# Layer 2's first down projection in seven products for four pairs of tiles, and seven tests moved

## The chip, the cores and the metric

One Trainium2 chip, of which the kernel uses one core. The metric is the device time of one execution, in microseconds (us). The engines are named as the profile names them: PE is the matrix engine (TensorE), DVE the vector engine, ACT the scalar engine, POOL the engine called GpSimd, SP the engine that issues most of the transfers. Each works through its own queue in the order in which the program was written; semaphores make one wait for another.

## The reference

Two layers, each a Fourier mixing step and a gated block, both added to x (2048 tokens of 640 features; the gated block has 1728 hidden features):

```python
x = x + _A_ref(_layernorm(x), dft_seq_re, dft_seq_im, dft_hid_re, dft_hid_im)
x = x + _B_ref(_layernorm(x), w_gate, w_up, w_down)
...
def _B_ref(x, w_gate, w_up, w_down):
    g = jnp.einsum("bsd,df->bsf", x, w_gate)
    u = jnp.einsum("bsd,df->bsf", x, w_up)
    h = _sigmoid(g) * u
    return jnp.einsum("bsf,fd->bsd", h, w_down)
```

`_A_ref` is Re(DFT_seq(DFT_hidden(x))) with the DFT matrices given as inputs. The change touches the last product of `_B_ref`, called "down" here, and the place of some work on the inputs.

## The kernel before, in words

**Precision.** Each operand is kept as two 16-bit parts, high and low, and each product is made of three matmuls (high by high, high by low, low by high). To make the parts of a value, ACT writes the high one and DVE the low one as the difference.

**Blocks, tiles and steps.** The tokens are worked on in four blocks of 512 (b = 0 to 3), each of four row groups of 128. The hidden features make 13 tiles of 128 (j = 0 to 12) and a short one (j = 13, "the tail", 64 wide). For each block there is a stretch of gate and up products, one unit of steps for each tile (units 0 to 13 of the block), and then the down product in eight steps (units 14 to 21). The number of a job in the code, `block[0] + 13.6` for example, is a place in this count: it says between which matmuls the job is written, and so where it stands in the queue of its engine. It is no time.

**Gate and up.** `seven(b, j)` makes gate and up of two tiles with seven products for eight (a scheme of Strassen's kind: some operands are sums, and products serve several results). It interleaves four places for jobs (`some(0)` to `some(3)`) with its parts: `part_one` to `part_seven` are PE's, `gate` is ACT's sigmoid, `up` (L1600, L1602) DVE's two multiplications, `part_seven` and `part_three` end with DVE's L1572 and L1580, and `up_parts` splits the finished tile. The results of two tiles are finished only in the next step. The last call has tile 12 alone, works off what is left, and does the tail (`gate_tail`, L1726 to L1730).

**Down, plain.** `down` takes the row groups one after another: 14 tiles, three matmuls a tile (two for the tail), two column halves of 320: 328 matmuls for a block (L1743). Each half ends in an add to x on DVE (L1758).

**Down, in seven products.** Where `(layer, b)` is in `MADE`, tiles 2m and 2m+1 form a pair m (0 to 5), whose hidden features are a 2 by 2 matrix of halves of 256 tokens. `mated_down` multiplies it by the pair's weights with seven products, called A11, A12, A22 and S1 to S4. For that, `mates_sums` makes four sums of a pair (L1629 to L1632, DVE) and `mates_parts` splits them: hA for the products A11 and A12, hS for S1 and S2, hR for S3 and S4, hB for A22 (L1640 on ACT, L1641 on DVE; hB is 256 wide, the others 512). hA comes with the pair's second tile, the rest in `mates_rest` one step later; the last pair's rest is written behind the 38th entry of down. The products are chained in PSUM banks: A11 in bank "a" is added to x by DVE (L1808), then S2 goes on in the same bank, is added, then S3, then A22; S1 and S4 share bank "d" in the same way. A product that goes on in a bank must wait for the add before it. The tiles without a partner (12 and 13 before) go in as plain matmuls (L1799). In layer 2, blocks 1, 2 and 3 are done so: 252 + 40 = 292 matmuls a block. The pair's summed weights ("T", 640 KB a pair) are loaded by `load_t` on SP.

**Work that rides along.** In layer 2's block 0 the Fourier step's results for row groups q = 1 to 3 are still being put together on DVE: `combine` (L1288), `join_hidden` (L1302 or L1304, with L1214 and L1215) and `add_hidden` (L1323), six jobs for each q. During a block's down the next block's operands are prepared, for two pairs of row groups: `pair_apply` (L655), `pair_combine` (L662 to L665), `pair_parts` (L673 on ACT, L674 on DVE) and `pair_transpose` (SP, L680). The kernel relies on symmetries of the DFT matrices, and 84 **tests** check these on the inputs all through the program: POOL loads rows of `in_ct` (L1916: four transfers for a test), DVE folds them (L1922, L1923, L1925), ACT sums the squares (L1888). A tuple of `TESTS` is (layer, block, place of the load, of the folding, of the sum). Similar tests look at `in_wh`. Ten tests stood in the down of layer 1's last block, ten in layer 2's block 0.

**From layer to layer.** Layer 2 begins with the Fourier step. Its first products need the last rows of layer 1, by way of DVE's add (L1758), statistics, POOL, ACT and DVE again: L939 (ACT) and L949 (DVE) write what PE's L1088 reads.

Of the kernel before, what the change touches and what calls it, by code (L numbers as in the profile page):

```python
# [18 lines left out]
D = 640  # L19
# [61 lines left out]
NP = 6  # L81
MADE = {(1, 1), (1, 2), (1, 3)}
TESTS = [(0, 1, 3.5, 4.9, 5.7), (0, 1, 4.5, 5.9, 6.7), (0, 1, 5.5, 7.1, 7.9), (0, 1, 7.38, 8.97, 9.78), (0, 1, 9.25, 10.85, 11.65), (0, 1, 11.12, 12.72, 13.53),
# [195 lines left out]
def folded(ctx, tc, pool, dram, big, acc, flag, homes, x, ct, wh, wg, wu, wc, wd, out):  # L279
# [66 lines left out]
    def at(u, f, *a):  # L346
        jobs[max(0, int(u // 1))].append((u, f, a))
# [1302 lines left out]

    def seven(b, j, mated=False):

# [23 lines left out]
        def mm(some):  # L1676
            ps, k = bank() if last else (None, None)
            for i in js:
                part_one(b, i, mated and i < 2 * NP)
            for i in js:  # L1680
# [86 lines left out]

    def mated_down(b, store):

        accs = {}  # L1770
        last = b == NB - 1

        def left(m, q, hp, p):
# [8 lines left out]
        def products_of(p, n, q, w, start, stop):  # L1782
            out = [(m, hp, wp) for m in range(NP) for hp, wps in PASSES for wp in wps]

            def one(k, m, hp, wp):
                if (p, n) not in accs:
                    accs[p, n] = bank()
                nc.tensor.matmul(accs[p, n][0][:, :EH], left(m, q, hp, p), right(m, w, wp), start=start and k == 0,  # L1788
                                 stop=stop and k == len(out) - 1, skip_group_check=True)

            return [(one, k, *t) for k, t in enumerate(out)]

        def plain(p, n, g, e, start):
            out = [(j, hp, wp) for j in range(2 * NP, NF + 1) for hp, wps in (PASSES if j < NF else PASSES[:1]) for wp in wps]
# [22 lines left out]
        def done(name):  # L1817
            for m in range(NP):
                drop(name, 2 * m)
# [4 lines left out]
        for p in range(2):  # L1824
            todo += products_of(p, "c", A12, 1, True, False)
        todo += [(done, "hA")]
        for p in range(2):
            todo += products_of(p, "a", S2, 4, False, True) + [(add, p, "a", p, 1, False)]
        for p in range(2):
            todo += plain(p, "c", p, 0, False) + [(add, p, "c", p, 0, True)]  # L1830
            todo += [(put, p, slice(0, EH))] if last and p == GA else []
        for p in range(2):
            todo += products_of(p, "d", S1, 3, True, True) + [(add, p, "d", p + 2, 1, False)]
        todo += [(done, "hS")]
        for p in range(2):
            todo += products_of(p, "a", S3, 5, False, True) + [(add, p, "a", p + 2, 1, False)]
        for p in range(2):
            todo += plain(p, "e", p + 2, 1, True) + [(add, p, "e", p + 2, 1, True)]
            todo += [(put, p + 2, slice(EH, D))] if last and p + 2 == GD else []
        for p in range(2):  # L1840
            todo += products_of(p, "a", A22, 6, False, False) + plain(p, "a", p + 2, 0, False)
            todo += [(add, p, "a", p + 2, 0, True)] + ([(put, p + 2, slice(0, EH if last and p + 2 == GD else D))] if last or p else [])
            todo += [(done, "hB")] if p else []
            q = 1 - p
            todo += products_of(q, "d", S4, 2, False, False) + plain(q, "d", q, 1, False)
            todo += [(add, q, "d", q, 1, True)] + ([(put, q, slice(EH if last and q == GA else 0, D))] if last or p else [])
        marks = [n for n, t in enumerate(todo) if t[0].__name__ == "one"]
        cuts = [0] + [marks[len(marks) * k // 8] for k in range(1, 8)] + [len(todo)]

        def step(k):  # L1850
# [11 lines left out]
            def post():  # L1862
                if k < 7:
                    return
                done("hR")
                for j in range(2 * NP, NF + 1):
                    drop("ht", j)
# [238 lines left out]
    for layer in range(2):  # L2106
# [11 lines left out]
        for b in range(NB):  # L2118
            block.append(len(steps) - 3 * (b == 0))
            for j in range(3 * (b == 0), NF + 1):  # L2120
                plain = b == 0 and (first or j < 4)
                steps.append(gate_up(b, j) if plain else seven(b, j, (layer, b) in MADE) if j % 2 == 0 else None)
            if first and b == last:
# [8 lines left out]
            if (layer, b) in MADE:  # L2132
                steps += mated_down(b, not first)
        end = len(steps)
# [75 lines left out]
        for q in range(1, NB):  # L2210
            for n, (f, *a) in enumerate(((combine, 0), (combine, 1), (join_hidden, 0), (add_hidden, 0), (join_hidden, 1),
                                         (add_hidden, 1))):
                at(block[0] + 1.6 + 0.8 * n if q == 1 else block[0] + (9.6 if q == 2 else 15.6) + n, f, q, *a)
        for b in range(1, NB):
# [52 lines left out]
        for m in range(NP):  # L2267
# [7 lines left out]
            else:  # L2275
                at(block[1] + (7.6, 9.6, -3.4, -2.8, -2.2, 0.6)[m], load_t, m)
        for b in range(1, NB if first else 2):
            at(block[b] - 8.1, slots.now)
        if not first:
            at(block[1] - 8, slots.hole, XU + XTU, XTU)  # L2280
            for b in range(NB - 1):
# [205 lines left out]
```

## Time and profile before

| | |
|---|---|
| time, median of 3 runs | 1126.85 us (1126.62 to 1129.57) |
| the profiled execution | 1127.29 us, its span 1125.5 us |
| instructions in the span | 23738 |
| mean granted PE clock | 0.997 |
| HBM read, written | 180.90 MB, 29.37 MB |
| layer 2, block 0: the steps of `seven` | 657 to 713.5 us |
| layer 2, block 0: down | 713.5 to 758.1 us |
| layer 2, block 1: down | 839.1 to 878.8 us |
| layer 1, block 3: down | 553.5 to 598.1 us |

The span runs from the first to the last instruction of one profiled execution; the time of that execution is 1.8 us longer. Rows of the profile give a start, a duration, the engine, the line in the code and the operation; "out<-in" names the tiles, and nearly all of them are parts of one large buffer, "big", "acc" being a bank of PSUM. A bracket such as [0.92 <-ACT big L1616] says how long the engine stood idle before the row, and which instruction released it. In rows of a window (A:B) the columns are its length, the busy time of PE, PEld (PE's weight loads), DVE, ACT and POOL with their instructions, the granted clock of PE as a share of full speed, the share of the DMA engines' time and GB/s.

### The profile page before, as it was taken

How to read it: one execution, taken by the hardware profiler on the slowest of the kernel's cores; microseconds unless marked ns; L12 is line 12 of the kernel's file. 1: busy time of each engine (PE TensorE's matmuls, PEld its weight loads, DVE VectorE, ACT ScalarE, POOL GpSimd, SP SyncE). 2: the span in 40 equal slices, each digit the busy share in tenths (PEclk: the TensorE clock that was granted, in tenths of full speed). 3: DMA queues.
4: the chain of work that ended last, by engine and by line, in shares of the span. 5: the costliest groups of instructions: out<-in, count | busy, mean ns of one | idle time of the engine just before them, and what ended most of it. 6: DMA issues, size and time to landing. Idle time of an engine off the chain costs nothing. (4 is left out here: it accounts for less than half of the span.)

```text
span 1125.5 us, 23738 instructions
## 1 busy us (share of the span) xinstructions
PE 1104.8 (98%) x9004; PEld 881.6 (78%) x9004; DVE 827.2 (73%) x1841; ACT 532.0 (47%) x1153; POOL 345.7 (31%) x568
## 2 busy tenths in 40 slices
PE   7999999999999999999999999999999999999997
PEld 5767446788878887788877878778887888788875
DVE  7984987868877898686568877864887398827962
ACT  6975584245534654255434734422652255415530
POOL 1001654342555445243480202433530214011001
PEclk9999999999999999999999999999999999999999
DMA  7533886889598969977761674598857873398401
GB/s 237 196 103 105 303 295 208 256 260 297 204 220 245 284 208 223 266 258 240 188 200 34 183 201 160 141 254 293 258 153 157 297 244 80 99 259 232 156 7 45
DMA packets 158050, 226.54 MB, mean 201 GB/s; under 512 B 75055, under 2 KB 100161, under 8 KB 157926
## 3 DMA queue, kind: packets, MB, share of 16 engines
q1 hardware_dynamic: 139222, 176.84, 52.3%
q0 software_dynamic: 18560, 47.93, 14.8%
q8 instruction: 72, 1.18, 0.4%
q14 instruction: 52, 0.43, 0.1%
q10 hardware_dynamic: 144, 0.16, 0.0%
HBM read 180.90 MB, written 29.37 MB: 187 GB/s over the span
## 5 line engine op out<-in xcount | busy, mean ns | idle before, releaser
L1531 PE MATMUL acc<-big 128*128 128x256 f16 x4698 | 516.8, 273 | 0.8 <-DMA big<-kept_w 0.4
L1531 PEld LDWEIGHTS <-big 128*128 128x128 f16 x4698 | 459.6, 98 | 55.6 <-issue 0.8
L1916 POOL DMA_DIRECT2D big<-in_ct x256 | 174.3, 687 | 209.5 <-DVE big L1925 121.4
L1743 PE MATMUL acc<-big 128*128 128x320 f16 x1640 | 223.6, 299 | 0.0
L1535 ACT ACTIVATE big<-acc 128x256 f32<-128x256 f32 x268 | 100.7, 381 | 231.4 <-PE acc L1531 220.8
L1743 PEld LDWEIGHTS <-big 128*128 128x128 f16 x1640 | 160.5, 98 | 62.2
L1888 ACT ACTIVATE big<-big 128x768 f32<-128x768 f32 (+9 forms) x110 | 81.3, 739 | 77.6 <-DVE big L1925 61.8
L1484 PE MATMUL acc<-big 128*128 128x256 f16 (+1 forms) x705 | 114.7, 325 | 0.3 <-ACT big L730 0.3
L1788 PE MATMUL acc<-big 128*128 128x320 f16 x756 | 105.6, 299 | 0.0
L1484 PEld LDWEIGHTS <-big 128*128 128x128 f16 x705 | 68.9, 98 | 44.9 <-issue 0.6
L1788 PEld LDWEIGHTS <-big 128*128 128x128 f16 x756 | 74.0, 98 | 28.6
L323 DVE SCALAR_TENSOR_TENSOR big<-big 128x640 f16<-128x640 f32 (+8 forms) x88 | 72.1, 848 | 15.7 <-ACT big L321 10.0
L1589 ACT ACTIVATE big<-big 128x512 f32<-128x512 f32 x87 | 52.8, 628 | 63.1 <-DVE big L1580 62.8
L321 ACT ACTIVATE big<-big 128x640 f16<-128x640 f32 (+8 forms) x88 | 58.6, 698 | 24.6 <-POOL big L1390 10.9
L1600 DVE SCALAR_TENSOR_TENSOR big<-acc,big 128x256 f32<-128x256 f32 x87 | 36.3, 418 | 43.2 <-PE acc L1531 38.6
L1617 DVE TENSOR_TENSOR big<-big 128x512 f16<-128x512 f32 x51 | 35.2, 689 | 42.0 <-ACT big L1616 41.1
L1580 DVE TENSOR_TENSOR big<-big,acc 128x512 f32<-128x512 f32 x87 | 56.2, 679 | 3.2 <-PE acc L1531 2.9
L1808 DVE SCALAR_TENSOR_TENSOR big<-acc,big 128x320 f32<-128x320 f32 x48 | 23.0, 487 | 44.7 <-PE acc L1799 33.1
L494 POOL DMA_INDIRECT out<-big,rows x8 | 8.8, 1105 | 140.5 <-DMA out<-big 53.5
L1641 DVE TENSOR_TENSOR big<-big 128x512 f16<-128x512 f32 x72 | 41.2, 617 | 9.9 <-ACT big L1640 9.9
L673 ACT ACTIVATE big<-big 128x384 f16<-128x384 f32 (+2 forms) x48 | 28.6, 647 | 41.3 <-DVE big L655 29.2
L1572 DVE TENSOR_TENSOR big<-acc,big 128x256 f32<-128x256 f32 x80 | 30.4, 415 | 23.8 <-PE acc L1531 20.8
(268 smaller groups left out, 1312.4 us busy)
## 6 DMA issues: line engine op xcount, KB each, us to landing
big<-kept_s SPq DMA_DIRECT2D x84, 512.0 KB
big<-kept_w SPq DMA_DIRECT2D x115, 320.0 KB
big<-in_ct POOLq DMA_DIRECT2D x256, 128.0 KB, 5.2
big<-kept_w SPq DMA_DIRECT2D x74, 192.0 KB
kept_w<-big SPq DMA_DIRECT2D x27, 320.0 KB
big<-in_ct POOLq DMA_DIRECT2D x32, 256.0 KB, 5.7
big<-in_wd SPq DMA_DIRECT2D x25, 320.0 KB
kept_s<-big SPq DMA_DIRECT2D x13, 512.0 KB
```

Source lines behind the costliest of these rows:

```text
L321: nc.scalar.activation(dh, src, AF.Copy, scale=s)
L323: nc.vector.scalar_tensor_tensor(dl, src, s, dh, op0=OP.mult, op1=OP.subtract)
L1484: nc.tensor.matmul(ps, w[wp][:, d * P : (d + 1) * P], xt[:, xp, :], start=(d == 0 and wp == HI and xp == HI), stop=(d == ND - 1 and wp == LO))
L1531: nc.tensor.matmul(ps, wt, xt, start=start and n == 0, stop=n == len(todo) - 1, skip_group_check=not start)
L1535: nc.scalar.activation(dst, ps, AF.Copy)
L1580: nc.vector.tensor_tensor(v[1], v[1], both, op=OP.add)
L1589: nc.scalar.activation(v, v, AF.Sigmoid, scale=SG)
L1641: nc.vector.tensor_tensor(l, src, h, op=OP.subtract)
L1743: nc.tensor.matmul(held["pd", e][0][:, :EH], held["ht", j].parts[hp][:, i * P : (i + 1) * P], held["w", 2, j].parts[wp][:, e * EH : (e + 1 ...
L1788: nc.tensor.matmul(accs[p, n][0][:, :EH], left(m, q, hp, p), right(m, w, wp), start=start and k == 0, stop=stop and k == len(out) - 1, ski ...
L1888: nc.scalar.activation(v, v, AF.Square, accum_out=new_sum()[:p])
L1916: nc.gpsimd.dma_start(v[:, g], bass.AP(ct.tensor, (r * S + row) * S, [[P, NS], [d * S, 16], [1, P]]))
```

## The change

Layer 2's block 0 joins the blocks whose down is made in seven products, for the pairs 2 to 5 alone (tiles 4 to 11); tiles 0 to 3, 12 and 13 stay single. In this block the singles' products are placed between the products that go on in one bank (behind A12 and behind S1), and the last products come in another order (both S4 first, then both A22). The summed weights of pairs 2 to 5 are loaded earlier, into room that is opened for it during the block; the block's rows are stored as in the other blocks done so, two of the row groups after the end of down. The next block's operands are prepared at the places that go with this kind of down, a little later in the order. The hidden step's jobs for q = 3 in layer 2 stand two places earlier (13.6 to 18.6 for 15.6 to 20.6). Of the ten tests in layer 1's last down four go, and the six that stay stand further apart; of five in the gate and up steps of layer 2's block 0 three go; seven stand now in block 1's down.

```diff
-MADE = {(1, 1), (1, 2), (1, 3)}
+MADE = {(1, 0): range(2, NP), (1, 1): range(NP), (1, 2): range(NP), (1, 3): range(NP)}
...
-         ... (0, 3, 15.6, 16.3, 16.8), (0, 3, 16.1, 16.8, 17.3), (0, 3, 16.6, 17.3, 17.8),
-         (0, 3, 17.1, 17.8, 18.3), (0, 3, 17.6, 18.3, 18.8), (0, 3, 18.1, 18.8, 19.3), (0, 3, 18.6, 19.3, 19.8), (0, 3, 19.1, 19.8, 20.3), (0, 3, 19.6, 20.3, 20.8),
-         (0, 3, 20.1, 20.8, 21.3), (1, 0, 6.0, 8.0, 8.8), (1, 0, 7.4, 9.4, 10.2), (1, 0, 8.8, 10.8, 11.6), (1, 0, 10.2, 12.2, 13.0), (1, 0, 11.6, 13.6, 14.4),
+         ... (0, 3, 15.6, 16.6, 17.1), (0, 3, 16.4, 17.4, 17.9), (0, 3, 17.2, 18.2, 18.7),
+         (0, 3, 18.0, 19.0, 19.5), (0, 3, 18.8, 19.8, 20.3), (0, 3, 19.6, 20.6, 21.1), (1, 0, 7.0, 9.0, 9.8), (1, 0, 10.0, 12.0, 12.8), ...
+         ... (1, 1, 14.0, 15.7, 16.6), (1, 1, 15.0, 16.7, 17.6), (1, 1, 16.0, 17.7, 18.6), (1, 1, 17.0, 18.7, 19.6),
+         (1, 1, 18.0, 19.7, 20.6), (1, 1, 19.0, 20.7, 21.6), (1, 1, 20.0, 21.7, 22.6), ...
...
-                part_one(b, i, mated and i < 2 * NP)
+                part_one(b, i, i // 2 in pairs)
...
-    def mated_down(b, store):
+    def mated_down(b, store, pairs):
...
+        single = [j for j in range(NF + 1) if j // 2 not in pairs]
...
+        singles = [], []
+        for p in range(2):
+            singles[0].extend(plain(p, "c", p, 0, False) + [(add, p, "c", p, 0, True)])
...
+        for p in range(2):
+            singles[1].extend(plain(p, "e", p + 2, 1, True) + [(add, p, "e", p + 2, 1, True)])
...
+        if b == 0:
+            todo += singles[0]
         for p in range(2):
             todo += products_of(p, "a", S2, 4, False, True) + [(add, p, "a", p, 1, False)]
+        if b:
+            todo += singles[0]
         for p in range(2):
             todo += products_of(p, "d", S1, 3, True, True) + [(add, p, "d", p + 2, 1, False)]
         todo += [(done, "hS")]
+        if b == 0:
+            todo += singles[1]
         for p in range(2):
             todo += products_of(p, "a", S3, 5, False, True) + [(add, p, "a", p + 2, 1, False)]
+        if b:
+            todo += singles[1]
+        ends = [], []
         for p in range(2):
...
+            if b:
+                todo += ends[0] + ends[1]
+                ends = [], []
+        todo += ends[1] + ends[0]
...
-                at(block[0] + 1.6 + 0.8 * n if q == 1 else block[0] + (9.6 if q == 2 else 15.6) + n, f, q, *a)
+                at(block[0] + 1.6 + 0.8 * n if q == 1 else block[0] + (9.6 if q == 2 else 15.6 if first else 13.6) + n, f, q, *a)
...
-                at(block[1] + (7.6, 9.6, -3.4, -2.8, -2.2, 0.6)[m], load_t, m)
+                at(block[1] + (7.6, 9.6, -11, -7.9, -7.6, -8.7)[m], load_t, m)
...
+            at(block[0] + 3, slots.hole, XU + XTU, FT * 2)
+            at(block[1] - 8, slots.close, XU + XTU)
```

More of the change, by code (lines that the diff above doesn't have):

```diff
@@ L1649, in mates_rest, with seven @@
             drop("hs", j)
-    def seven(b, j, mated=False):
+    def seven(b, j, pairs=()):
         js = [j, j + 1] if j + 1 < NF else [j]
@@ L1782, in products_of @@
         def products_of(p, n, q, w, start, stop):
-            out = [(m, hp, wp) for m in range(NP) for hp, wps in PASSES for wp in wps]
+            out = [(m, hp, wp) for m in pairs for hp, wps in PASSES for wp in wps]
             def one(k, m, hp, wp):
@@ L1793, in plain @@
         def plain(p, n, g, e, start):
-            out = [(j, hp, wp) for j in range(2 * NP, NF + 1) for hp, wps in (PASSES if j < NF else PASSES[:1]) for wp in wps]
+            out = [(j, hp, wp) for j in single for hp, wps in (PASSES if j < NF else PASSES[:1]) for wp in wps]
             def one(k, j, hp, wp):
@@ L1817, in done @@
         def done(name):
-            for m in range(NP):
+            for m in pairs:
                 drop(name, 2 * m)
@@ L1826, in mated_down @@
         todo += [(done, "hA")]
+        singles = [], []
+        for p in range(2):
+            singles[0].extend(plain(p, "c", p, 0, False) + [(add, p, "c", p, 0, True)])
+            singles[0].extend([(put, p, slice(0, EH))] if last and p == GA else [])
+        for p in range(2):
+            singles[1].extend(plain(p, "e", p + 2, 1, True) + [(add, p, "e", p + 2, 1, True)])
+            singles[1].extend([(put, p + 2, slice(EH, D))] if last and p + 2 == GD else [])
+        if b == 0:
+            todo += singles[0]
         for p in range(2):
             todo += products_of(p, "a", S2, 4, False, True) + [(add, p, "a", p, 1, False)]
-        for p in range(2):
-            todo += plain(p, "c", p, 0, False) + [(add, p, "c", p, 0, True)]
-            todo += [(put, p, slice(0, EH))] if last and p == GA else []
+        if b:
+            todo += singles[0]
         for p in range(2):
@@ L1834, in mated_down @@
         todo += [(done, "hS")]
+        if b == 0:
+            todo += singles[1]
         for p in range(2):
             todo += products_of(p, "a", S3, 5, False, True) + [(add, p, "a", p + 2, 1, False)]
+        if b:
+            todo += singles[1]
+        ends = [], []
         for p in range(2):
[L1838 to L1843, printed above, removed]
-            q = 1 - p
-            todo += products_of(q, "d", S4, 2, False, False) + plain(q, "d", q, 1, False)
-            todo += [(add, q, "d", q, 1, True)] + ([(put, q, slice(EH if last and q == GA else 0, D))] if last or p else [])
+            ends[0].extend(products_of(p, "a", A22, 6, False, False) + plain(p, "a", p + 2, 0, False))
+            ends[0].extend([(add, p, "a", p + 2, 0, True)])
+            ends[0].extend([(put, p + 2, slice(0, EH if last and p + 2 == GD else D))] if last or p else [])
+            ends[0].extend([(done, "hB")] if p else [])
+            q = 1 - p
+            ends[1].extend(products_of(q, "d", S4, 2, False, False) + plain(q, "d", q, 1, False))
+            ends[1].extend([(add, q, "d", q, 1, True)])
+            ends[1].extend([(put, q, slice(EH if last and q == GA else 0, D))] if last or p else [])
+            if b:
+                todo += ends[0] + ends[1]
+                ends = [], []
+        todo += ends[1] + ends[0]
         marks = [n for n, t in enumerate(todo) if t[0].__name__ == "one"]
@@ L1865, in post @@
                 done("hR")
-                for j in range(2 * NP, NF + 1):
+                for j in single:
                     drop("ht", j)
@@ L2121, in folded @@
                 plain = b == 0 and (first or j < 4)
-                steps.append(gate_up(b, j) if plain else seven(b, j, (layer, b) in MADE) if j % 2 == 0 else None)
+                steps.append(gate_up(b, j) if plain else seven(b, j, MADE.get((layer, b), ())) if j % 2 == 0 else None)
             if first and b == last:
@@ L2132, in folded @@
             if (layer, b) in MADE:
-                steps += mated_down(b, not first)
+                steps += mated_down(b, not first, MADE[layer, b])
         end = len(steps)
```

10 rows, old and new, of the table TESTS are left out of this document.

## The prediction

> **What bounds the kernel now.** I read the first part of the profile's page, then the chain that ended last, then TensorE's waits after the opening, then VectorE in order of time.
>
> ```profile
> PE 1104.8 (98%) x9004; PEld 881.6 (78%) x9004; DVE 827.2 (73%) x1841; ACT 532.0 (47%) x1153; POOL 345.7 (31%) x568
> 713.71 44.55 PE acc L1743 x328
> PE acc L1088 <- ACT big L939: 1.4, 1, 1.4
> PE acc L1531 <- DMA big<-kept_w: 0.4, 1, 0.4
> ```
>
> TensorE is busy 98% of the span, and after the opening hardly anything makes it wait. So a matmul less is worth its slot, as long as nothing new makes TensorE wait. The second row is the stage that changes: layer 2's first down, 328 matmuls in 44.55 us, 0.1358 us each. But a 98% engine hides how close the next one is. VectorE (DVE) has 73% over the span, and around this down it has no rest:
>
> ```profile
> 687.92 0.69 DVE L1617 TENSOR_TENSOR big<-big 128x512 f16<-128x512 f32 x1 [3.77 <-ACT big L1616]
> ...
> 701.59 0.75 DVE L1572 TENSOR_TENSOR big<-acc,big 128x256 f32<-128x256 f32 x2
> ...
> 712.72 0.69 DVE L1617 TENSOR_TENSOR big<-big 128x512 f16<-128x512 f32 x1 [0.92 <-ACT big L1616]
> 713.44 0.69 DVE L1727 SCALAR_TENSOR_TENSOR big<-acc,big 64x512 f32<-64x512 f32 x1
> ...
> 715.53 0.83 DVE L1304 SCALAR_TENSOR_TENSOR big<-big 128x644 f32<-128x644 f32 x1
> ...
> 717.33 0.42 DVE L1922 TENSOR_TENSOR big<-big 128x256 f32<-128x256 f32 x1
> ...
> 718.53 0.42 DVE L1578 TENSOR_TENSOR big<-big 128x256 f32<-128x256 f32 x1
> ...
> 721.93 0.69 DVE L1617 TENSOR_TENSOR big<-big 128x512 f16<-128x512 f32 x1 [0.74 <-ACT big L1616]
> ```
>
> From 687.92 to 712.72 nothing but the queue itself sets when an instruction starts (the one other wait there is 0.19). The last row makes the low half of tile 12, ready at 722.6. Down starts at 713.55 and reads it at its 73rd matmul, at 723.3: 0.7 us to spare, 8 us after down began. VectorE is already that far behind TensorE.
>
> **The change part by part.** *Matmuls.* Four pairs by seven products: 7 x 2 halves x 4 pairs x 3 passes = 168. Singles: five full tiles x 3 + 2 = 17, on 4 row groups x 2 column halves = 136. Together 304, 24 fewer: **-3.26 us**. The mixed kind of down issues at the same slot in block 1 (108 matmuls in 14.67 us by the chain), so this term is sure; the counts follow from the loops, and that the change leaves them as they were is no case to weigh.
>
> *VectorE's queue in layer 2, block 0.* Prices, from block 1, which does all this today:
>
> ```profile
> 843.68 0.42 DVE L1629 TENSOR_TENSOR big<-big 128x256 f32<-128x256 f32 x1
> ...
> 845.14 0.41 DVE L1600 SCALAR_TENSOR_TENSOR big<-acc,big 128x256 f32<-128x256 f32 x1
> ...
> 847.24 0.88 DVE L1808 SCALAR_TENSOR_TENSOR big<-acc,big 128x320 f32<-128x320 f32 x2
> 848.04 1.62 DVE L1641 TENSOR_TENSOR big<-big 128x512 f16<-128x512 f32 x3
> 849.58 1.13 DVE L655 TENSOR_SCALAR big<-big,small 128x640 f32<-128x640 f32 x2
> ...
> 852.35 1.75 DVE L674 TENSOR_TENSOR big<-big 128x384 f16<-128x384 f32 x3
> ```
>
> From start to start: a pair's four sums 1.46, its three late parts (hS, hR, hB) 1.54, an add 0.40, apply and combine of a row pair of the next block 2.77, its first three parts 1.67. From the first fence: a test 1.20, a join 1.80, the tail 2.09 with its wait; a combine is two additions of 128x322, 0.8. Of the 1.54, a 512 part is 0.60 and the 256 part 0.34; hA and the part of a tile that isn't paired are 512 parts too, an up is two halves of 0.33.
>
> Now the queue, in the order of the code. In the step of tiles 8 and 9, three parts (1.54) stand at 687.9 for a part and an up (1.28): 0.26 late. In the step of tiles 10 and 11, sums and parts come (3.00), a test and a half-tile part go (1.80): 1.5 late, so the L1572 of 701.59 ends tile 10 at 703.4. TensorE needs that at 704.1: still no wait. In tile 12's step another 1.46 of sums comes, tile 10's half-tile part goes (0.8 with its wait): tile 11's up, which ended at 711.8 (712.72 less the wait of 0.92), ends at 713.8. Three parts (1.54) and hA (0.60) follow: the pair 10/11's hA is ready at 715.9. The first product reads its low half at its 12th matmul, at 715.0: **0.9**.
>
> Then tail 2.09, join 1.80, the combine moved up to 13.6 (0.8, for a test of 1.20 that goes), 1.05 for L1578 and L1580, sums 1.46, up 0.67, a wait on ACT of 0.71: tile 12's high half at 724.3, its low half at 725.0. The singles, now in front of S2, read it at matmuls 61 and 63: 722.6. **2.1** (1.7 and 0.4).
>
> From 725.0 these stand ahead of the add that ends S2: two adds 0.8, late parts 1.54, combine 0.8, L1323 pair 1.54, apply and combine 2.77, test 1.20, join 1.80, parts 1.67, test 1.20, fourth part 0.87, two adds 0.8; with the add itself 15.4: 740.4. TensorE reaches S3, which goes on in the same bank, 102 matmuls after 725.0, at 738.9: **1.5**; the second half finds another L1323 pair ahead of its add: **0.3**. S4 waits likewise for S1's second add, behind apply and combine (2.77) and an add: 745.8 against 743.9: **1.9**. After that it is even. In all **+6.7**, so this stage ends 3.5 later, not 3.3 earlier. Bounds: 0, if the queue is reached earlier by as much as it is lengthened; 10, if waits on reused room, which no row shows, come on top. I take the walk, since by the same walk the rows of before come out within half a microsecond.
>
> *ACT and the transfers.* ACT has one 512 and one 256 activation more per pair and is idle half of this stage: nothing. Four loads of the paired weights (640 KB each, on SP) go from 750 and 765 to before and about the start of down:
>
> ```profile
> 710.00:720.00 10.00, 10.00 (x79) 7.56 (x78) 7.69 (x16) 4.21 (x9) 5.42 (x12) 1.00 0.30 99
> ```
>
> They come into a stretch at DMA share 0.30 and are first read at about 728, so they cost nothing; without cover one costs the 3 us that 640 KB take at 200 GB/s. They leave the stretch after 750, at whose end TensorE waits 0.4 for weights (first fence): **-0.4** (0 to -0.4). Stores of the block's rows come later, behind all this.
>
> *Seven tests out of layer 1's end and this block, into block 1's down.* Two places. First, the end of layer 1, where four of ten tests go:
>
> ```profile
> 574.87 16.16 POOL L1916 DMA_DIRECT2D big<-in_ct  x24
> 601.11 0.47 DVE L1758 SCALAR_TENSOR_TENSOR big<-acc,big 128x320 f32<-128x320 f32 x1
> 599.65 6.07 PE L1088 MATMUL acc<-big 128*128 128x256 f16 x54
> 607.13 0.39 PE L1088 MATMUL acc<-big 128*128 128x256 f16 x2 [1.42 <-ACT big L939]
> 608.02 3.05 PE L1088 MATMUL acc<-big 128*128 128x256 f16 x16 [0.50 <-DVE big L949]
> 605.00:610.00 5.00, 2.97 (x21) 1.79 (x19) 4.14 (x10) 3.25 (x8) 0.00 (x0) 0.92 0.01 3
> 610.00:615.00 5.00, 5.00 (x41) 3.95 (x39) 3.84 (x8) 4.09 (x10) 0.00 (x0) 0.74 0.00 0
> ```
>
> The last add (601.11) runs 2.8 us after its product (598.1 plus 0.2), because VectorE's queue is full of tests whose data POOL issues at 2.7 us a test until 591. Everything up to L939 and L949 hangs on that add. Four tests fewer are 4.8 of VectorE and 10.8 of POOL: the add comes on time, both waits end 2.8 earlier, before TensorE gets there at 605.7. That gives back 2.1 (605.7 to 608.0, less two matmuls). The granted clock then fell (0.92 and 0.74 in these slices, 5 x 0.08 + 5 x 0.26 = 1.7 us lost), because of this hole; that goes too. 3.8, of which I take **-3.5**, since a small wait may show up behind (bounds 0, if the queue stays late, and -4.1).
>
> A rule speaks on the clock. The Trainium skill (TensorE: Matmul & The Clock Gate, Part 1) has the clock drop after a whole idle window of about 3.4 us. By it a hole of 2.1 us would cost only itself, here and in the down, and the sum would lose 1.7 of that gain. The trace differs: the hole above held two matmuls and the clock still fell.
>
> Second, block 1's down:
>
> ```profile
> 861.18 1.29 DVE L674 TENSOR_TENSOR big<-big 128x384 f16<-128x384 f32 x2 [1.97 <-DMA big<-big]
> 864.52 1.07 DVE L1808 SCALAR_TENSOR_TENSOR big<-acc,big 128x320 f32<-128x320 f32 x2
> 866.26 2.61 PE L1788 MATMUL acc<-big 128*128 128x320 f16 x18
> ```
>
> Three tests (3.6) come ahead of S3's add at 864.52, with an idle 1.97 to take them up: 1.6 late or more, against 1.3 to spare before the matmul of 866.26. **+0.8** (0 to 2.3, the latter if the idle moves along).
>
> **Sum:** -3.26 + 6.7 - 0.4 - 3.5 + 0.8 = +0.3. The profiled execution took 1127.29 (span 1125.5 and 1.8 around it), so 1127.6; the median shown is 0.44 lower than that execution: **1127.1**.
>
> **Rivals.** (1) *VectorE keeps up*: the down's holes don't come, the rest does: -3.26 - 0.4 - 3.5, 1119.7. For it: the kernel's holds elsewhere cost nothing at 0.7 spare; in block 1 hA comes 1.4 after the start of down and still in time. Against: there fewer additions stand in tile 12's step, and six pairs give hA 15 matmuls, four only 9. Half of the holes gives 1123.0. (2) *Slower: tests' data late.* VectorE waits for the data of the last tests of this down, with the adds of S3 now queued behind:
>
> ```profile
> 742.24 0.42 DVE L1923 TENSOR_TENSOR big<-big 128x256 f32<-128x256 f32 x1 [2.38 <-DMA big<-in_ct]
> 748.46 0.43 DVE L1923 TENSOR_TENSOR big<-big 128x256 f32<-128x256 f32 x1 [1.56 <-DMA big<-in_ct]
> ```
>
> Before, only adds with a whole product's time to spare stood behind such waits. If both recur ahead of S3's adds, which are just in time, that is 4 more: 1131.1. It decides where data land after VectorE gets to them, about 746 and 752. Against: VectorE gets there later than before. (3) *The clock halves in the down*, after the 2.1 or the 1.9: 1.7 each; the first is taken up by the waits behind it, the second not: 1128.8, and 1130.5 if another follows.
>
> **How the numbers follow.** Forecast 0.40; rival 1 0.28; rival 2 0.20; rival 3 0.12, a third of it beyond 0.3%. About 0.3% (3.4 us) is what a measurement here tells from no change: faster means below 1123.5, slower above 1130.2. So faster 0.28, same 0.48, slower 0.24. The forecast's own range is 1124 to 1130; with most of rivals 1 and 2, and with the layer's end giving nothing back (1130.6), the range is 1120 to 1133.
>
> **What would show it.** Right: 304 matmuls in layer 2's first down, four holes there, before the third pair's end of A11, in the first singles, at S3 and at S4, put down to L1641, L1616/L1617 and L1808; no wait on L939 and no half clock near 605 to 613; VectorE busy without rest from 689 to 746. Wrong: a down of 41.3 us with no hole, or the hole at 607 still there.

## The result, and the profile after

The changed kernel takes **1152.53 us** (median of 4 runs, 1148.93 to 1155.01), the kernel before 1126.73 in the same series (4 runs): ratio **1.0228, 95% interval 1.0212 to 1.0244**, slower, and far above the upper end of the forecast range (1133). The profiled execution took 1150.57 us, its span 1148.7, that is 23.2 us more than the 1125.5 of before. TensorE's waits in that span, longest sum first (engine, tile, line, what it waited for: us in total, times, longest):

```profile
PE acc L1531 <- ACT big L1535: 7.9, 3, 6.6
PE acc L1789 <- DVE big L1809: 6.8, 2, 4.8
...
PE acc L1531 <- DMA big<-big: 4.4, 1, 4.4
PE acc L1800 <- ACT big L1616: 1.9, 1, 1.9
```

(In the changed kernel the product of a pair is L1789, a single's L1800, the add to x L1809, tile parts L1616, L1617 as before.) Before, TensorE's longest wait after the opening was 1.4 us. To see where the waits lie, I cut both spans at the first product of each stage of layer 2; lengths in us:

| stage | before | after | difference |
|---|---|---|---|
| Fourier step, from L1088 on | 57.60 | 53.49 | -4.1 |
| block 0, down | 44.55 | 48.73 | +4.2 |
| block 1, steps | 81.00 | 88.85 | +7.9 |
| block 1, down | 39.66 | 47.55 | +7.9 |
| block 2, steps | 79.91 | 86.28 | +6.4 |
| block 3, steps | 80.14 | 81.19 | +1.1 |

The other stages differ by 0.3 or less. The stage that was rewritten lost 4.2; **22.1 us were lost in three stages whose own matmuls the change leaves alone**. Three places follow, each shown by TensorE and by what released it.

**Block 0's down.** TensorE in order of time (start, us, engine, line, operation, tiles, count, idle before and who ended it), then slices of 5 us with the columns explained under "Time and profile before":

```profile
711.47 5.20 PE L1789 MATMUL acc<-big 128*128 128x320 f16 x37 [0.43 <-DVE big L1641]
...
720.20 0.45 PE L1800 MATMUL acc<-big 128*128 128x320 f16 x2 [1.89 <-ACT big L1616]
720.92 4.56 PE L1800 MATMUL acc<-big 128*128 128x320 f16 x20 [0.28 <-DVE big L1617]
...
741.96 1.79 PE L1789 MATMUL acc<-big 128*128 128x320 f16 x12 [2.06 <-DVE big L1809]
```

```profile
605.00:610.00 5.00, 5.00 (x50) 4.23 (x48) 4.75 (x11) 3.81 (x11) 0.00 (x0) 1.00 0.01 3
...
720.00:725.00 5.00, 4.52 (x20) 2.55 (x21) 4.83 (x10) 1.49 (x4) 0.00 (x0) 0.66 0.01 3
...
740.00:745.00 5.00, 3.04 (x23) 2.20 (x23) 4.83 (x12) 2.25 (x5) 0.68 (x1) 1.00 0.99 295
```

Four holes, 4.66 us together. Behind the second and third the granted clock is 0.66 in the slice: twenty matmuls took 4.56 us for 2.72 (0.1358 each). The first slice is the end of the layer change, where before stood 0.92 and a hole: now 1.00 and none.

**Block 1's steps.** First ACT in the kernel before, then SP, POOL, ACT and TensorE of the changed kernel, picked in order of time:

```profile
768.78 0.38 ACT L1535 ACTIVATE big<-acc 128x256 f32<-128x256 f32 x1 [4.20 <-PE acc L1531]
```

```profile
759.68 1.29 SPq L499 DMA_DIRECT2D out<-big  x2
...
768.49 1.11 POOL L494 DMA_INDIRECT out<-big,rows  x1 [21.45 <-DVE big L1580]
772.26 0.98 POOL L494 DMA_INDIRECT out<-big,rows  x1 [2.66 <-issue]
...
778.64 0.66 ACT L1535 ACTIVATE big<-acc 128x256 f32<-128x256 f32 x2 [13.93 <-DMA out<-big,rows]
779.08 6.09 PE L1531 MATMUL acc<-big 128*128 128x256 f16 x39 [6.60 <-ACT big L1535]
```

Before, ACT's copy waited 4.20 us, for TensorE's product alone. Now ACT stood idle for 13.93 us until a store of block 0's rows had landed: its copy of a product goes into room that these rows had held. TensorE stood idle for 6.60 of that, because its bank came free too late (last row); the slices 770 to 780 and 780 to 790 then show a granted clock of 0.79 and 0.87.

**Block 1's down and block 2's start.** The kernel before and then the changed one: SP's transpositions of the next block's operands, VectorE and TensorE.

```profile
853.33 5.08 SPq L680 DMA_TRANSPOSE big<-big  x2
861.57 10.55 SPq L680 DMA_TRANSPOSE big<-big  x2
...
878.76 26.47 PE L1531 MATMUL acc<-big 128*128 128x256 f16 x241
```

```profile
861.11 7.08 SPq L680 DMA_TRANSPOSE big<-big  x2
871.40 17.60 SPq L680 DMA_TRANSPOSE big<-big  x2
...
873.83 1.29 DVE L674 TENSOR_TENSOR big<-big 128x384 f16<-128x384 f32 x2 [4.50 <-DMA big<-big]
...
878.91 4.96 PE L1789 MATMUL acc<-big 128*128 128x320 f16 x18 [4.79 <-DVE big L1809]
898.97 6.20 PE L1531 MATMUL acc<-big 128*128 128x256 f16 x42 [4.36 <-DMA big<-big]
```

```profile
880.00:885.00 5.00, 5.00 (x21) 2.76 (x20) 2.41 (x8) 1.88 (x4) 4.16 (x7) 0.51 1.30 153
```

The down begins at 839.10 before and 846.79 after, so the first pair of transpositions is issued at the same place (14.2 and 14.3 us into the stage). But VectorE's next L674, which overwrites what they read, is released 7.9 us after their issue before (861.18) and 12.7 after. The second pair is handed out over 17.60 us for 10.55, and its data are in place only 27.6 us after its own issue began (898.97); before it was at most 17.2 us, since block 2 started without a wait at 878.76. Each of the two holes is followed by a slow stretch, 0.51 in the slice behind the first.

### The profile page after: what moved, and what is told of

It is laid out like the page before. It is cut to its first block, busy times and chain, and to the rows that moved or that the text cites. A ratio compares the mean times of both kernels' runs of the same rounds, so it can differ in the third digit from the quotient of the medians.

```text
span 1148.7 us, 23714 instructions
## 1 busy us (share of the span) xinstructions
PE 1108.7 (97%) x8980; PEld 881.2 (77%) x8980; DVE 839.5 (73%) x1873; ACT 533.7 (46%) x1161; POOL 346.6 (30%) x568
## 5 line engine op out<-in xcount | busy, mean ns | idle before, releaser
L1531 PEld LDWEIGHTS <-big 128*128 128x128 f16 x4698 | 461.2, 98 | 69.3 <-issue 13.5
L1933 POOL DMA_DIRECT2D big<-in_ct x256 | 174.9, 689 | 208.2 <-DVE big L1942 102.2
L1535 ACT ACTIVATE big<-acc 128x256 f32<-128x256 f32 x268 | 99.6, 381 | 224.0 <-PE acc L1531 200.5
L1743 PE MATMUL acc<-big 128*128 128x320 f16 x1312 | 178.9, 299 | 0.0
L1743 PEld LDWEIGHTS <-big 128*128 128x128 f16 x1312 | 128.4, 98 | 49.8
L1789 PE MATMUL acc<-big 128*128 128x320 f16 x924 | 132.3, 302 | 7.3 <-DVE big L1809 6.8
L1789 PEld LDWEIGHTS <-big 128*128 128x128 f16 x924 | 91.1, 99 | 44.7 <-issue 7.5
L1905 ACT ACTIVATE big<-big 128x768 f32<-128x768 f32 (+9 forms) x110 | 81.5, 741 | 93.5 <-DVE big L1942 66.0
L1484 PEld LDWEIGHTS <-big 128*128 128x128 f16 x705 | 68.9, 98 | 44.9 <-issue 0.6
L1809 DVE SCALAR_TENSOR_TENSOR big<-acc,big 128x320 f32<-128x320 f32 x64 | 30.1, 486 | 40.5 <-PE acc L1800 29.0
L1580 DVE TENSOR_TENSOR big<-big,acc 128x512 f32<-128x512 f32 x87 | 56.3, 680 | 3.4 <-PE acc L1531 3.2
L1641 DVE TENSOR_TENSOR big<-big 128x512 f16<-128x512 f32 x88 | 50.4, 617 | 10.4 <-ACT big L1640 10.4
L1617 DVE TENSOR_TENSOR big<-big 128x512 f16<-128x512 f32 x43 | 29.7, 690 | 32.8 <-ACT big L1616 32.0
L1950 POOL DMA_DIRECT2D big<-in_ct x40 | 27.5, 691 | 71.2 <-ACT big L1535 44.7
```

Source lines behind the costliest of these rows:

```text
L1484: nc.tensor.matmul(ps, w[wp][:, d * P : (d + 1) * P], xt[:, xp, :], start=(d == 0 and wp == HI and xp == HI), stop=(d == ND - 1 and wp == LO))
L1531: nc.tensor.matmul(ps, wt, xt, start=start and n == 0, stop=n == len(todo) - 1, skip_group_check=not start)
L1535: nc.scalar.activation(dst, ps, AF.Copy)
L1580: nc.vector.tensor_tensor(v[1], v[1], both, op=OP.add)
L1641: nc.vector.tensor_tensor(l, src, h, op=OP.subtract)
L1743: nc.tensor.matmul(held["pd", e][0][:, :EH], held["ht", j].parts[hp][:, i * P : (i + 1) * P], held["w", 2, j].parts[wp][:, e * EH : (e + 1 ...
```

## The experiments

Twelve kernels; "A", "B" and "C" name the three places: the seven tests of block 1's down, the stores of block 0's rows, VectorE's queue in block 0's down. Stage lengths (us) from each profiled run:

| run | Fourier | b0 down | b1 steps | b1 down | b2 steps | b3 steps | median time | ratio to before (95%) |
|---|---|---|---|---|---|---|---|---|
| e1 | 53.49 | 48.54 | 87.72 | 39.67 | 79.91 | 81.89 | 1142.17 | 1.0131 (1.0115 to 1.0148) |
| e2 | 53.49 | 48.52 | 90.66 | 46.31 | 86.81 | 80.91 | 1152.85 | 1.0229 (1.0211 to 1.0246) |
| e3 | 53.50 | 44.55 | 80.12 | 46.01 | 86.62 | 79.97 | 1135.05 | 1.0065 (1.0048 to 1.0082) |
| e4 | 53.50 | 44.55 | 80.10 | 39.67 | 79.91 | 79.97 | 1125.49 | 0.9981 (0.9971 to 0.9990) |
| e5 | 53.50 | 48.53 | 86.10 | 47.31 | 85.92 | 80.64 | 1149.98 | 1.0210 (1.0193 to 1.0227) |
| e6 | 54.82 | 50.82 | 80.30 | 39.66 | 79.91 | 82.35 | 1142.30 | 1.0153 (1.0123 to 1.0183) |
| e7 | 53.49 | 46.27 | 80.09 | 39.66 | 79.91 | 80.86 | 1140.90 | 1.0130 (1.0113 to 1.0147) |
| e8 | 53.49 | 44.56 | 80.21 | 39.67 | 79.91 | 80.07 | 1123.29 | 0.9969 (0.9958 to 0.9980) |
| e9 | 53.48 | 48.91 | 80.85 | 40.00 | 92.97 | 81.09 | 1143.11 | 1.0143 (1.0125 to 1.0162) |
| e10 | 53.48 | 50.12 | 87.72 | 43.75 | 87.09 | 80.67 | 1151.40 | 1.0232 (1.0198 to 1.0265) |
| e11 | 53.48 | 50.12 | 90.48 | 39.99 | 79.91 | 82.32 | 1139.18 | 1.0103 (1.0079 to 1.0128) |
| e12 | 53.48 | 48.49 | 81.47 | 39.66 | 79.91 | 86.35 | 1136.79 | 1.0076 (1.0051 to 1.0101) |

### A: the seven tests alone, and without them (e1, e3)

e1, the changed kernel with

```diff
-(1, 1, 14.0, 15.7, 16.6), (1, 1, 15.0, 16.7, 17.6), (1, 1, 16.0, 17.7, 18.6),
+(1, 3, 10.6, 12.1, 12.8), (1, 3, 11.3, 12.8, 13.5), (1, 3, 12.0, 13.5, 14.2),
...
```

> The changed kernel with its seven tests of block 1's down moved behind block 3's step of tile 10 (seven places in block 3 of layer 2), nothing else touched. Theory A: these tests, by their transfers and by their 1.2 us each on VectorE, make the hole of 4.8 us in block 1's down, the half clock behind it and the late transposition at block 2's start; without them block 1's down goes from 47.6 back to about 39.7 us and block 2's steps from 86.3 to about 80, so -14.3: about 1138 us. Rival A': the down in seven products with its own later preparation makes them late; then the two holes stay and the time stays at 1150 or above.

1142.17 us. Block 1's down and block 2's steps are back at 39.67 and 79.91: 7.88 + 6.37 = 14.25 regained, as expected. The time fell by only 10.4, because the tests cost something at their new place: block 3's down, behind them, took 42.70 us for 39.82 (four holes of 0.21 to 0.89), and its steps 0.7 more.

e3, the kernel before with the changed kernel's list of tests:

```diff
-         (0, 3, 17.1, 17.8, 18.3), (0, 3, 17.6, 18.3, 18.8), (0, 3, 18.1, 18.8, 19.3),
...
+         (1, 1, 18.0, 19.7, 20.6), (1, 1, 19.0, 20.7, 21.6), (1, 1, 20.0, 21.7, 22.6),
```

> The kernel before with the changed kernel's list of tests and nothing else of the change (so four out of layer 1's end, three out of block 0's steps, seven into block 1's down). Theory A says that the seven cost the same 14.3 us beside the old down of block 0, and layer 1's end gives 4.3 back: about 1136.7 us. If the seven only hurt together with the new down, layer 1's end alone is seen: about 1122.4 us.

1135.05 us. With the old down of block 0 the two holes are there in full (4.63 and 3.91 us): block 1's down 6.4 longer, block 2's steps 6.7, 13.1 together; the Fourier step gives 4.1 and block 1's steps 0.9. So the seven tests need nothing else of the change to do their harm.

### A: VectorE's time or the transfers (e10, e11)

A test is transfers (POOL), folds (VectorE) and a sum (ACT). e10 keeps the transfers, e11 the folds (there `new_room` stands for `load`, and `fold_only`, VectorE's four instructions, at place v); `room_back` gives the room free:

```diff
-            if l == layer:
+            if (l, b) == (1, 1) == (layer, 1) and u >= 14:
+                at(block[b] + u, load, *key)
+                at(block[b] + w, room_back)
+            elif l == layer:
```

> The changed kernel in which the seven tests of block 1's down only load their rows; VectorE's folding and ACT's sums of these seven are left out. Theory A1 (transfers): they slow the transpositions; block 2's start keeps its hole of 4.4 us and the clock behind it (+6.4), the down keeps the 2.5 us by which L674 waits longer, less the slack of 1.3 us: down near 41 us, in all about 1146 us. Theory A2 (VectorE's time): both holes go, 1138 us.

> The changed kernel in which the seven tests of block 1's down load nothing: VectorE folds what lies in their rooms, ACT's sums of these seven are left out. Theory A1 (transfers): the transpositions take their old time, block 2 starts without a hole, and the down keeps a hole of some 2 us for 4.8 us of folds ahead of S3's add: about 1142 us. Theory A2 (VectorE's time): the down's hole of 4.8 us stays and block 2's start with it, 1150 us or more.

e11 first: 1139.18 us, down 39.99, block 2's steps 79.91. Its transpositions, and the only thing left of the hole:

```profile
864.39 5.54 SPq L680 DMA_TRANSPOSE big<-big  x2
...
872.51 1.28 DVE L674 TENSOR_TENSOR big<-big 128x384 f16<-128x384 f32 x2
...
873.21 9.96 SPq L680 DMA_TRANSPOSE big<-big  x2
...
877.58 2.60 PE L1789 MATMUL acc<-big 128*128 128x320 f16 x18 [0.17 <-DVE big L1809]
```

L674 no longer waits at all, and the folds cost 0.3 us, less than the 2 expected. e10 took 1151.40 us (1147.60 in the profiled run):

```profile
870.59 1.29 DVE L674 TENSOR_TENSOR big<-big 128x384 f16<-128x384 f32 x2 [3.19 <-ACT big L673]
...
871.66 21.06 SPq L680 DMA_TRANSPOSE big<-big  x2
...
890.92 0.37 PE L1531 MATMUL acc<-big 128*128 128x256 f16 x1 [3.79 <-DMA big<-big]
896.50 8.75 PE L1531 MATMUL acc<-big 128*128 128x256 f16 x63 [5.21 <-DMA big<-big]
```

The transfers alone make down and steps 4.1 and 7.2 longer (3.79 of the first is the hole at block 2's first product), 11.3 of the 14.3. About 3 us need both: in e10 L674 was released 9.0 us after the first issue (861.59), not 12.7, and TensorE has no hole at S3. In the changed kernel POOL's loads wait for a fold or a sum to free their room and go out beside the transposition until 871.84, while in e10 those ahead of L674 are all out by 863.32; that this makes the difference is likely, not shown. The transfers by queue show how the first transposition was stretched, 861 to 874 of the changed kernel and then 853 to 862 of the kernel before (queue: packets, MB, share of the 16 engines' time):

```profile
q1 hardware_dynamic: 4637, 1.76, 74.1%
q0 software_dynamic: 240, 0.66, 24.8%
```

```profile
q1 hardware_dynamic: 4656, 1.84, 90.2%
```

SP's queue (q1) moves about the same, in 13 us for 9, because POOL's (q0) has a quarter of the engines' time beside it (24.8% of 13 us is 3.2 of the 4 us). That fits the Trainium skill (DMA: Bandwidth & Descriptors, Queues, rings and completion order), by which each DMA engine takes a packet in turn from every queue that has work: a second busy queue takes its share from the transposition.

### B: the stores (e2, e5, e9)

e2:

```diff
-at(block[b + 1] + 1.3, store_x, b, g, slice(0, D))
+at(block[b + 1] + (1.3 if b else 0.0), store_x, b, g, slice(0, D))
```

> The changed kernel with the stores of block 0's row groups GB and GC written at block 1's start instead of 1.3 units later, so that they no longer stand behind VectorE's L1580; the order on every engine is the same. Theory B: ACT's snaps wait for these stores to leave the room that they reuse (hole of 6.6 us and half clock); the stores then start some 8 us earlier, at about 760, and block 1's steps go from 88.9 back to about 81 us: -7.9, about 1144.6 us. Rival B': the weights, whose loads wait for the same room and whose transfers are crowded, are the next thing late: -2 at most, about 1150.5 us.

1152.85 us, no change, and the store left no earlier:

```profile
769.94 1.11 POOL L494 DMA_INDIRECT out<-big,rows  x1 [22.46 <-DVE big L1580]
```

So the releaser that the row names, L1580, was not what it waited for, and theory B in this form fell. SP's two stores of the other row groups had been issued ten microseconds earlier, behind six loads of weights. e5 turned the order round:

```diff
-            ends[0].extend([(put, p + 2, slice(0, EH if last and p + 2 == GD else D))] if last or p else [])
+            ends[0].extend([(put, p + 2, slice(0, EH if last and p + 2 == GD else D))] if last or p and b else [(put, GC, slice(0, D)), (put, GA, slice(0, D)), (put, GD, slice(0, D))] if p else [])
...
-            ends[1].extend([(put, q, slice(EH if last and q == GA else 0, D))] if last or p else [])
+            ends[1].extend([(put, q, slice(EH if last and q == GA else 0, D))] if last or p and b else [] if p or b else [(put, GB, slice(0, D))])
...
-                for g in (GB, GC) if made else ():
+                for g in (GB, GC) if made and b else ():
```

> The changed kernel with the four stores of block 0's rows in another order: GB behind its last add, then at the end of down GC, GA, GD (GB and GC by POOL, GA and GD by SP); nothing else. Theory B2, formed after the store's earlier place changed nothing: every write to the output waits for the one before it to land, GA's and GD's on SP now come first and land some 8 us after their issue, behind six loads of weights, and GB's and GC's, into whose room ACT's snaps go, wait for them. With GB and GC first the hole of 6.6 us and the half clock go: -7.9, about 1144.6 us. Rival: the weights' loads, which also wait for this room, are then the next late thing: -2 at most, 1150 us or more.

1149.98 us, the rival's time but not its reason:

```profile
758.71 1.11 POOL L494 DMA_INDIRECT out<-big,rows  x1 [11.74 <-DVE big L1809]
766.75 0.97 POOL L494 DMA_INDIRECT out<-big,rows  x1 [6.93 <-DVE big L1572]
...
769.80 0.81 SPq L499 DMA_DIRECT2D out<-big  x2
...
776.17 0.66 ACT L1535 ACTIVATE big<-acc 128x256 f32<-128x256 f32 x2 [10.90 <-DMA out<-big]
```

Now POOL's first store leaves at 758.71 (0.8 us after the end of down, for 10.6 before), and SP's wait for both of POOL's: POOL's stores, which are indirect ones (their rows are looked up), and SP's wait for each other, while SP's own two go out together (0.81 us for both). But ACT's wait only changed its partner, from "out<-big,rows" (POOL's) to "out<-big" (SP's), and the hole went from 6.60 to 3.57: the kernel's own planner, which gives every tile its stretch of the buffer, had laid ACT's tile (units 12 to 20) over the rows of GC and GD (10 to 20), and one of them is always last in such a chain. So e9 left the stores and opened the room a step later:

```diff
-at(block[b + 1] + (1.4 if made else 0.9), slots.hole, 20 * b, 20)
+at(block[b + 1] + (2.4 if b == 0 else 1.4 if made else 0.9), slots.hole, 20 * b, 20)
```

> The changed kernel with the room of block 0's rows opened to other tiles one step later (2.4 for 1.4 behind block 1's start), so that ACT's snaps of block 1's second step are given other room; stores, their order and the tests as they are. Theory B3: the stores cost only through that one tile, which lies over GC's and GD's room: the hole of 6.6 us in block 1's steps and the half clock behind it go, -7.9, about 1144.6 us. Rival: the next tiles that go into this room, weights of steps 5 and 6 by SP, wait in its place and hold SP's queue: -2 at most, 1150 us.

1143.11 us, 9.4 less. Block 1's steps: 80.85, no hole, so the stores cost through this one tile. The planner's rooms moved elsewhere too, and with them A's harm: the down lost its hole and block 2 got one of 9.28.

```profile
881.42 2.70 POOL L1933 DMA_DIRECT2D big<-in_ct  x4 [18.04 <-DMA big<-big]
...
889.93 0.43 DVE L1939 TENSOR_TENSOR big<-big 128x256 f32<-128x256 f32 x1 [16.23 <-DMA big<-in_ct]
...
892.10 0.84 ACT L1905 ACTIVATE big<-big 128x768 f32<-128x768 f32 x1 [19.38 <-DVE big L1942]
892.94 0.64 ACT L1535 ACTIVATE big<-acc 128x256 f32<-128x256 f32 x2
893.36 6.88 PE L1531 MATMUL acc<-big 128*128 128x256 f16 x41 [9.28 <-ACT big L1535]
```

Read upwards: ACT's copies (L1535), which free TensorE's banks, stand behind a test's sum (L1905); that waits for the fold, that for the rows, and POOL could load them only when a transposition had let go of the room. Down and steps together are 13.4 longer than in the kernel before, much the same price as in the changed kernel (14.3) by another road.

### C: block 0's down, and both repairs together (e6, e7, e12)

e6 has e5's order and the seven tests at layer 1's block 3 (`(0, 3, 5.00, 6.40, 7.20)` and so on by 1.0); e7 also moves the five tests of block 0's down to layer 1's blocks 1 and 2:

```diff
-(1, 0, 14.0, 15.4, 16.0), ... (1, 0, 15.0, 16.4, 17.0), (1, 0, 16.0, 17.4, 18.0),
+(0, 1, 0.50, 1.90, 2.70), ... (0, 1, 1.50, 2.90, 3.70), (0, 1, 2.50, 3.90, 4.70),
...
```

> The order of stores of the run before, and besides the seven tests of block 1's down moved to layer 1's block 3 (steps 5 to 11). If theories A and B2 both hold and add up, -14.3 and -7.9: about 1130.3 us; with A alone about 1138.2 us.

> The run before, and besides the five tests of block 0's down moved to layer 1's blocks 1 and 2. Theory C: VectorE's queue makes the holes of block 0's down; 6 us less of it ahead of S1's second add take the hole of 2.06 us at S4 away, while the one at tile 12 (1.89 and 0.28) stays, since none of the five stands ahead of it: -2.1, about 1128.2 us. Rival: the hole at S4 hangs on the data or on apply and combine, and stays: about 1130.3 us.

1142.30 and 1140.90 us. Both lost early what they won late: layer 2's first product comes at 608.96 and 611.49 instead of 599.42, since the tests made waits of up to 3.4 us in layer 1's steps. Behind that, all three stages of A and B are as before (80.3, 39.66, 79.91). In e6 the planner had put ACT's tile elsewhere, so it doesn't tell order from room; in e7 it lay where it was, and the copies still waited for the stores, 5.44 us, of which 4.20 is idle in any case. For C, e7's down:

```profile
732.26 0.45 PE L1800 MATMUL acc<-big 128*128 128x320 f16 x2 [1.89 <-ACT big L1616]
732.99 4.56 PE L1800 MATMUL acc<-big 128*128 128x320 f16 x20 [0.28 <-DVE big L1617]
...
748.53 5.05 PE L1789 MATMUL acc<-big 128*128 128x320 f16 x36
```

The hole at S4 is gone (36 matmuls without a break), the one at tile 12 unchanged to the hundredth: as VectorE's queue has it. But the stage, 46.27, is still 1.7 longer than the old down of 44.55.

e12 joins e9's edit with four of the seven tests in layer 1's block 3 and three early in layer 2's block 3:

```diff
-(1, 1, 14.0, 15.7, 16.6), (1, 1, 15.0, 16.7, 17.6),
+(0, 3, 6.00, 7.40, 8.20), (0, 3, 7.00, 8.40, 9.20),
...
-(1, 1, 18.0, 19.7, 20.6), (1, 1, 19.0, 20.7, 21.6), (1, 1, 20.0, 21.7, 22.6),
+(1, 3, 0.80, 2.40, 3.20), (1, 3, 1.70, 3.30, 4.10), (1, 3, 2.60, 4.20, 5.00),
```

> The changed kernel with the room opened later as in the run of that name, and the seven tests of block 1's down at other places: four in layer 1's block 3 (steps 6 to 9), three in layer 2's block 3 (steps 0.8 to 2.6). Theories A and B3 add up: -14.3 and -7.9, about 1130.3 us, with 48.7 us left in block 0's down and no other loss. Rival: one of the two hides behind the other, or the places cost something: 1134 us or more.

1136.79 us. The repairs do add up: block 1's steps 81.47, its down 39.66, block 2's steps 79.91, 21.6 regained of 22.1. But the moved tests cost about 4.5 us in layer 1 and 5 in block 3 (holes of 2.23 and 1.06 there), so the time is the rival's.

### Layer 1's end alone (e4, e8)

e4 and e8 are the kernel before with the six tests of layer 1's last down spaced as in the changed kernel, and the other four elsewhere: late in layer 2's block 3 (e4, places 10.6 to 12.7), in layer 1's block 3 (e8, shown).

```diff
-(0, 3, 18.6, 19.3, 19.8), (0, 3, 19.1, 19.8, 20.3), (0, 3, 19.6, 20.3, 20.8), ... (0, 3, 20.1, 20.8, 21.3),
+(0, 3, 6.00, 7.40, 8.20), (0, 3, 7.00, 8.40, 9.20), (0, 3, 8.00, 9.40, 10.20), ... (0, 3, 9.00, 10.40, 11.20),
```

> The kernel before with four of the ten tests of layer 1's last down moved behind block 3's step of tile 10 of layer 2, the other six spaced as in the changed kernel, nothing else. If the gain of 4.3 us before block 0's down is theirs, about 1122.4 us, with no hole at layer 2's first products and no half clock there. Rival: the four cost in block 3 what they give at the layer's end, about 1126.5 us.

> The kernel before with four of the ten tests of layer 1's last down moved to layer 1's block 3 (steps 6 to 9), the other six spaced as in the changed kernel. Layer 1's end gives 4.1 back, and in the steps of block 3 VectorE has 30 to 50% to spare: 1122.7 us. Rival: the tests cost there what they cost at the end, about 1126.7 us.

Both regain the 4.1 us of the Fourier step. e4 gives 2.9 of it back in block 3's down (42.76), where VectorE and ACT now hold TensorE up (four holes of 0.23 to 0.94): 1125.49. e8 keeps it: **1123.29 us, ratio 0.9969 (0.9958 to 0.9980)**: 0.3% below the kernel before and the fastest kernel here, with nothing of the new down in it.

## Why the prediction was wrong

It gave 1127.1 us and a range to 1133; the kernel takes 1152.53.

- *Matmuls, VectorE's queue* (-3.26 and +6.7, the stage +3.5): the stage is +4.2. The walk placed three of the holes (0.9, 2.1 and 1.9 forecast; 0.43, 2.17 and 2.06 found). The one at S3 (1.5 and 0.3) isn't in the profiled run. Instead came half clock behind tile 12 (1.8), the mechanism of rival 3. The wait at S3 shows as 1.3 in exactly the five runs whose clock held behind tile 12 (e2, e6, e9, e10, e12); as rival 3 said, the waits behind it take the half clock up: the stage took 48.73 us with it and 48.52 without (e2). Holes and half clock add up to 6.5 us, but the stage is 7.4 longer than 24 matmuls fewer would make it; most of the rest is that rows of TensorE overlap by some 0.17 us when nothing waits (the row of 741.96 lasts 1.79, and the next begins at 743.58), which each hole loses too. e7 shows that the queue is the cause at S4. Mechanism right, size near.
- *Layer 1's end* (-3.5): -4.1, hole and half clock both gone, by itself in e3, e4 and e8. Right.
- *The -0.4* for weights at 780: that wait is gone, but in a stage that lost 7.9.
- *"Three tests (3.6) come ahead of S3's add at 864.52, with an idle 1.97 to take them up"* (+0.8): **wrong, +14.3**. This step priced the seven tests by VectorE's time alone. e11 shows that time at 0.3 us. Their 26 transfers (six tests of four and one of two, as tests on columns have) had no term. With them the idle that was to take the tests up grew from 1.97 to 4.50 (3.19 with the transfers alone, e10), and the second transpositions were late for block 2. The upper bound (2.3, "if the idle moves along") rested on the same omission.
- *"Stores of the block's rows come later, behind all this"* (no cost): **wrong, +7.9**. The step looked at the queues, not at the room that the stores hold: two went behind the end of down, POOL's stores and SP's wait for each other (e5), and a tile of the next block uses the rows' room (e9).
- *Rival 2*, tests' data late, was the nearest in kind. In its own stage such a wait came too late to hold TensorE up (VectorE waited 4.45 for such data at 756.66, with four last adds behind it); what the tests' transfers delayed lay one block later, and it was the transpositions. That VectorE keeps up (rival 1) is excluded.

Open: how much of B's delay is SP's transfers queued behind weights and how much the transfers' share; what block 0's down would take with tile 12's singles placed later, which wasn't tried; and the 1.1 us in block 3's steps, where one wait of 1.10 us on ACT is new. e9 moved other tiles as well, so that the one tile is the cause rests on e9 together with e6, where it also lay elsewhere.

## What to carry to other kernels

A step that is moved takes its transfers with it: ask what is in flight at the new place, above all transpositions, before asking whether the engine has time. When a result is stored later, look for the next owner of its room and for other stores to the same tensor; the first copy into that room is where it will be paid. And filler work is worth a trial by itself: here four tests taken from the layer's end made the fastest kernel of all (e8), without the new down.

## What was unexpected

- With POOL's loads of 128 KB beside SP's transposition, the time from its issue to the release of its source grew from 7.9 to 12.7 us (9.0 in e10), and the landing of the second one from at most 17.2 us after its issue to 27.6.
- The same holes had different sequels. Behind 1.89 and 0.28 us with two matmuls between, the clock fell in the changed kernel, e1, e5, e7 and e11, and held in e2, e6, e9, e10 and e12; behind 2.04 to 2.06 us without a matmul, at S4, it held in the changed kernel and fell in e6, e10 and e11. In the profiles' clock record the half-clock stretches of a run, but for the one at the end of the span, last one, two or three times 3.41 us and begin whole multiples of 3.41 us apart. These are slices of that raster: the kernel before, the changed kernel at 720 and at 740, and e2 at 720.

```profile
605.82:609.24 3.42, 1.49 (x11) 0.88 (x12) 3.19 (x9) 1.68 (x5) 0.00 (x0) 1.00 0.02 5
717.67:721.09 3.42, 1.24 (x9) 0.47 (x8) 2.63 (x7) 1.86 (x5) 0.00 (x0) 1.00 0.00 0
738.15:741.57 3.42, 1.75 (x13) 1.13 (x12) 3.35 (x8) 1.56 (x3) 0.94 (x2) 1.00 0.96 238
717.60:721.01 3.41, 1.52 (x12) 0.86 (x10) 2.62 (x8) 1.49 (x3) 0.00 (x0) 1.00 0.00 0
```

TensorE is idle for 1.93 and 2.18 us in the first two, behind which the clock fell, and for 1.67 and 1.89 us in the last two, behind which it held. In all fourteen profiles, after the opening, the clock fell behind every full-clock slice with at least 1.895 us of idle time and behind none with 1.892 or less (the ends of matmuls are modelled, so the edge may be less sharp). So in these runs the sequel of a hole hung on how much of it fell into one slice. The Trainium skill's rule (TensorE: Matmul & The Clock Gate, Part 1), a drop after a whole idle window of about 3.4 us, has the length of the slice; that all of it must be idle is not what these rows show.
- A row named VectorE's L1580 as the releaser of a store that waited for something else (e2). Where the named engine's work isn't an operand, suspect a coincidence of times.
